# Sliding-window attention followed by an MLP: flat 512-token MLP chunks, paired heads on the two array halves, wide exp and mask, norm ahead of the transpose

## The chip, the core and the metric

The kernel runs on one core of one Trainium2 chip. The metric is the device time of one execution in microseconds (us); less is better. The engines are named as in the profile: PE is TensorE (matmuls and transposes; PEld its weight loads), DVE is VectorE, ACT is ScalarE, POOL is GpSimd and SP is SyncE. [...] POOL and SP also issue the transfers (DMAs), whose packets all run on the same 16 DMA engines.

## The reference

Eight sequences (B = 8) of S = 576 tokens with H = 8 heads of D = 64, so the model width is 512. Attention is causal with a window of 128 and a bias by distance. Its output `x` goes through a layer norm and an MLP of 2048 hidden units, and is added to the result.

```python
scores = scale * np.matmul(q, k.transpose(0, 1, 3, 2))
mask = (rel >= 0) & (rel < window)
scores = np.where(mask, scores + bias[None], -1000000000.0)
...
attn = np.exp(scores)
attn = attn / (np.sum(attn, axis=-1, keepdims=True) + 1e-09)
return np.matmul(attn, v).astype(np.float32)
...
xn = (x - mu) / np.sqrt(var + 1e-06) * g_ln
ch = np.maximum(xn @ w_ch1, 0.0) @ w_ch2
return (x + ch).astype(np.float32)
```

## The kernel before

Tokens lie on the 128 partitions; a sequence of 576 tokens is four blocks of 128 and a tail of 64. The program runs in nine periods: period p does the attention of sequence p (`attn_gen`) and the MLP of sequence p - 1 (`mlp_main`). `drive` interleaves the two generators, and the framework's scheduler then settles each engine's order.

`stage_load` brings q, k and v of a sequence as 15 casting DMAs issued by POOL (fp32 in memory, fp16 on chip), two sequences ahead of need at the start and one ahead later. After the v load, DVE writes the column of ones of the v tile (line 111, `vx`); this write is queued on DVE and cannot run until that tile's transfers have landed.

Attention works on head pairs (`hp`, four a sequence). PE transposes q and k of two heads together (line 136, tile `ptr`), DVE copies them out (line 141, `qt` and `kt`). The scores of one head come from partitions 0 to 63 of these, those of the other from partitions 64 to 127 (line 155, tile `psc`, five matmuls a head, one head after the other). ACT takes the exp of at most 512 columns at a time (lines 163 and 176), DVE multiplies by a banded mask that also holds the bias (lines 169 and 182), and PE forms probabilities times v with a 65th column for the sum (lines 195 and 203, tile `ppv`). DVE normalises (lines 212 to 222) and takes statistics of each head (line 229).

`mlp_pre` combines the statistics on DVE (line 244), subtracts the mean (line 245) and computes the reciprocal root by integer arithmetic and two Newton steps (lines 254 to 285). `mlp_main` transposes (line 297, `pxc`), scales by `g_ln` while copying out on DVE (line 303, `xnt`), multiplies by `w1` for two halves of 288 tokens (line 317, 128 matmuls of 288 columns a sequence), applies relu on ACT or DVE in turn (lines 325 and 329, `ht`), and multiplies by `w2` for five token blocks (line 341, 16 matmuls of 512 columns a block, the last block only 64 tokens wide). DVE scales by the reciprocal root, adds `x` (line 349, `o_tile`), and SP stores.

Of the kernel before, what the change touches and what calls it, by code (L numbers as in the profile page):

```python
# [16 lines left out]
def kernel(  # L17
# [34 lines left out]
    for h in range(H):  # L52
# [21 lines left out]

    x_all = [
        xall_pool.tile([P, NSB, d_model], FP16, tag=f"x{b}", name=f"x_{b}")
        for b in range(B)
    ]

    stage_pool = ctx.enter_context(tc.tile_pool(name="stage", bufs=2))  # L80
    qt_pool = ctx.enter_context(tc.tile_pool(name="qtkt", bufs=2))
    probs_pool = ctx.enter_context(tc.tile_pool(name="probs", bufs=4))
    small_pool = ctx.enter_context(tc.tile_pool(name="small", bufs=4))
    xnt_pool = ctx.enter_context(tc.tile_pool(name="xnt", bufs=2))
    ht_pool = ctx.enter_context(tc.tile_pool(name="ht", bufs=1))
    xc_pool = ctx.enter_context(tc.tile_pool(name="xc", bufs=2))
    out_pool = ctx.enter_context(tc.tile_pool(name="outp", bufs=3))
    sm2_pool = ctx.enter_context(tc.tile_pool(name="sm2", bufs=2))
    att_psum = ctx.enter_context(tc.tile_pool(name="attps", bufs=4, space=bass.MemoryType.PSUM))
    m1_psum = ctx.enter_context(tc.tile_pool(name="m1ps", bufs=2, space=bass.MemoryType.PSUM))  # L90
    m2_psum = ctx.enter_context(tc.tile_pool(name="m2ps", bufs=2, space=bass.MemoryType.PSUM))

    staged = {}
    pre_state = {}

    def stage_load(b):
        qstage = stage_pool.tile([P, NSB, H, D], FP16, tag="qs", name=f"qs{b}")
        kstage = stage_pool.tile([P, NSB, H, D], FP16, tag="ks", name=f"ks{b}")
        vext = stage_pool.tile([P, NSB, H, D + 1], FP16, tag="vx", name=f"vx{b}")
        for src, dst in ((q, qstage), (k, kstage), (v, vext)):  # L100
            for sb in range(NSB):
                pb = pblk(sb)
                nc.gpsimd.dma_start(  # L103
                    out=dst[0:pb, sb, :, 0:D],
                    in_=src[b, :, sb * P : sb * P + pb, :].rearrange(
                        "h p d -> p h d"
                    ),
                )
        nc.vector.memset(qstage[TAIL:P, NSB - 1, :, :], 0.0)
        nc.vector.memset(kstage[TAIL:P, NSB - 1, :, :], 0.0)  # L110
        nc.vector.memset(vext[:, :, :, D : D + 1], 1.0)  # L111
        staged[b] = (qstage, kstage, vext)

    def load_weights():
        w1r = moe_w_ch1.rearrange("(kb p) f -> p kb f", p=P)
        for kb in range(NKB):
            nc.gpsimd.dma_start(out=w1sb[:, kb, :], in_=w1r[:, kb, :])
        w2r = moe_w_ch2.rearrange("(fb p) d -> p fb d", p=P)
        for f0 in range(0, NFB, 4):
            nc.gpsimd.dma_start(out=w2sb[:, f0 : f0 + 4, :], in_=w2r[:, f0 : f0 + 4, :])  # L120

    def attn_gen(b):
        qstage, kstage, vext = staged[b]
        xb = x_all[b]
        stats = sm2_pool.tile(
            [P, NSB, H, nc.vector.BN_STATS_DIM], FP32, tag="stats", name=f"st{b}"
        )
        pre_state[b] = stats
        nc.vector.memset(xb[TAIL:P, NSB - 1, :], 0.0)
        for hp in range(HPAIRS):  # L130
            qt = qt_pool.tile([P, NSB * P], FP16, tag="qt")
            kt = qt_pool.tile([P, NSB * P], FP16, tag="kt")
            for stg, dst in ((qstage, qt), (kstage, kt)):
                ptr = att_psum.tile([P, NSB * P], FP16, tag="att")
                for sb in range(NSB):
                    nc.tensor.transpose(  # L136
                        ptr[:, sb * P : sb * P + P],
                        stg[0:P, sb, 2 * hp : 2 * hp + 2, :],
                        iden[0:P, 0:P],
                    )  # L140
                nc.vector.tensor_copy(out=dst[:, :], in_=ptr[:, :])  # L141
                yield
            probs_2 = []
            for g in range(2):
                h = 2 * hp + g
                r0, r1 = 64 * g, 64 * g + 64
                probs = probs_pool.tile([P, NSB, 2 * P], FP16, tag="probs")
                probs_2.append(probs)
                for jb0 in range(0, NSB, 2):
                    njb = min(2, NSB - jb0)  # L150
                    psc = att_psum.tile([P, 2, 2 * P], FP32, tag="att")
                    for t in range(njb):
                        jbb = jb0 + t
                        nq = 2 * P if jbb < NSB - 1 else P
                        nc.tensor.matmul(  # L155
                            psc[:, t, 0:nq],
                            kt[r0:r1, jbb * P : jbb * P + P],
                            qt[r0:r1, jbb * P : jbb * P + nq],
                            start=True,
                            stop=True,  # L160
                        )
                    if njb == 2:
                        nc.scalar.activation(  # L163
                            out=probs[:, jb0 : jb0 + 2, :],
                            in_=psc[:, :, :],
                            func=AF.Exp,
                            scale=inv_sqrt_d,
                        )
# [191 lines left out]
    def drive(a_gen, b_gen, b_ratio):  # L360
        budget = 0.0
        while a_gen is not None or b_gen is not None:
# [6 lines left out]
            while b_gen is not None and budget >= 1.0:  # L369
                budget -= 1.0  # L370
                try:
                    next(b_gen)
                except StopIteration:
                    b_gen = None

    stage_load(0)
    stage_load(1)
    load_weights()

# [38 lines left out]
```

## Time and profile before

| what | value |
|---|---|
| time, median of 3 runs (lowest, highest) | 465.8 us (465.6, 467.54) |
| span of the profiled execution, first to last instruction | 462.7 us |
| PE busy in the span | 400.8 us (87%) |
| DVE busy | 317.5 us (69%) |
| ACT busy | 129.3 us (28%) |
| POOL busy | 106.4 us (23%) |
| mean granted TensorE clock | 0.954 |

The profiled execution has no time of its own beside its span; the median of the runs lies 3.1 us above that span, which is what lies around the first and the last instruction. Busy PE time is modelled and says little of how close PE is to its best; the starts of successive matmuls say more.

### The profile page before, as it was taken

The page shows a single profiled execution, that of the slowest core. Times are in us where ns is not written, and L with a number is a line of the kernel's source. Part 1 is how long each engine was busy: PE and PEld are TensorE (multiplying, and loading weights), DVE is VectorE, ACT ScalarE, POOL GpSimd, SP SyncE. Part 2 cuts the span into 40 slices and gives each one's busy share as a digit, 9 for nine tenths or more (in the row PEclk, how much of TensorE's full clock was granted, in tenths as well). Part 3 has the DMA queues.
Part 4 walks back from the last instruction along what each step waited for, and adds up shares of the span by engine and source line. Part 5 has one row for each costly group of instructions (what it writes and reads, how often), then busy time and mean ns, then how long its engine had stood idle before and what let it go on. Part 6 is the DMA issues. An engine that isn't in the chain of part 4 may idle for free.

```text
span 462.7 us, 8169 instructions
## 1 busy us (share of the span) xinstructions
PE 400.8 (87%) x3040; PEld 246.4 (53%) x3040; DVE 317.5 (69%) x1362; ACT 129.3 (28%) x321; POOL 106.4 (23%) x132
## 2 busy tenths in 40 slices
PE   1466829996999969997999969997999989998996
PEld 0244516643675447653676447653676456644752
DVE  3469826757787677757778678757878697758331
ACT  1242304500453024420463024420364034500310
POOL 9973510442007300343007300243000000000000
PEclk9999987998899979999799989999799999999999
DMA  9999990599009900299009930299000110011011
GB/s 145 134 161 207 173 54 0 40 135 85 1 1 114 121 24 1 16 134 108 2 1 85 126 47 1 18 133 107 3 1 1 69 36 0 1 70 34 1 45 59
DMA packets 121304, 28.88 MB, mean 62 GB/s; under 512 B 113968, under 2 KB 116016, under 8 KB 121264
## 3 DMA queue, kind: packets, MB, share of 16 engines
q0 software_dynamic: 115200, 18.36, 60.2%
q1 hardware_dynamic: 6064, 10.00, 6.4%
q8 instruction: 24, 0.39, 0.4%
q14 instruction: 16, 0.13, 0.1%
HBM read 37.26 MB, written 9.44 MB: 101 GB/s over the span
## 4 chain that ended last, share of the span: by engine, by line
PE 68%; DMA 11%; POOL 9%; DVE 7%; ACT 2%; issue 2%; POOLq 0%; DVEq 0%
PE psc L155 7%; PE ppv L195 4%; PE ppv L203 3%; DMA ks_544<-in_k_dram 2%; DVE xnt L303 2%; DMA vx_545<-in_v_dram 2%; DMA vx_143<-in_v_dram 2%; DVE o_tile L349 1%; PE pxc L297 1%; ACT ht L325 1%; DMA vx_3477<-in_v_dram 1%; PE ptr L136 1%; DMA vx_1278<-in_v_dram 1%; DMA vx_2011<-in_v_dram 1%; DMA vx_4210<-in_v_dram 1%
## 5 line engine op out<-in xcount | busy, mean ns | idle before, releaser
L317 PEld LDWEIGHTS <-w1sb 128*128 128x128 f16 x1024 | 97.2, 101 | 55.7 <-issue 24.6
L163 ACT ACTIVATE probs<-psc 128x512 f16<-128x512 f32 x128 | 70.5, 603 | 164.4 <-PE psc L155 163.4
L341 PEld LDWEIGHTS <-ht 128*128 128x128 f16 (+1 forms) x640 | 61.7, 100 | 61.3 <-issue 3.4
L169 DVE TENSOR_TENSOR probs<-probs,mband 128x512 f16<-128x512 f16 x128 | 52.1, 419 | 31.9 <-ACT probs L163 26.0
L155 PE MATMUL psc<-qt,kt 64*128 64x256 f16 (+1 forms) x320 | 48.4, 295 | 9.4 <-DVE kt L141 6.8
L155 PEld LDWEIGHTS <-kt 64*128 64x128 f16 x320 | 24.6, 102 | 27.2 <-issue 10.9
L297 PE MATMUL pxc<-iden,xcb 128*128 128x128 f16 (+1 forms) x160 | 16.9, 244 | 23.7 <-DVE xnt L303 21.4
L195 PEld LDWEIGHTS <-probs 128*128 128x128 f16 (+1 forms) x320 | 27.5, 103 | 15.7 <-DVE vx_122 L111 3.2
L303 DVE TENSOR_SCALAR xnt<-pxc,g_sb 128x128 f16<-128x128 f16 (+1 forms) x160 | 32.1, 261 | 0.0
L297 PEld LDWEIGHTS <-xcb 128*128 128x128 f16 (+1 forms) x160 | 11.2, 109 | 31.3 <-issue 27.9
L203 PEld LDWEIGHTS <-probs 128*128 128x128 f16 x256 | 22.8, 105 | 3.0
L141 DVE COPY qt<-ptr 128x640 f16<-128x640 f16 x32 | 15.1, 472 | 7.9 <-PE ptr L136 7.9
L176 ACT ACTIVATE probs<-psc 128x128 f16<-128x128 f32 x64 | 18.8, 294 | 0.0
L141 DVE COPY kt<-ptr 128x640 f16<-128x640 f16 x32 | 15.2, 476 | 3.0 <-PE ptr L136 3.0
L182 DVE TENSOR_TENSOR probs<-probs,mband 128x128 f16<-128x128 f16 x64 | 13.8, 216 | 0.0
L103 POOL DMA_DIRECT2D qs_2742<-in_q_dram x5 | 4.2, 865 | 34.0 <-PE ptr L136 34.0
L212 DVE RECIPROCAL rec<-ppv 128x4 f32<-128x4 f32 x64 | 10.9, 171 | 1.5 <-PE ppv L203 1.4
L103 POOL DMA_DIRECT2D qs_2009<-in_q_dram x5 | 4.2, 856 | 33.1 <-PE ptr L136 33.1
L103 POOL DMA_DIRECT2D qs_4208<-in_q_dram x5 | 4.2, 865 | 32.6 <-PE ptr L136 32.6
L103 POOL DMA_DIRECT2D qs_3475<-in_q_dram x5 | 4.2, 865 | 32.6 <-PE ptr L136 32.6
L136 PE MATMUL ptr<-iden,qs_120 128*128 128x128 f16 x20 | 3.6, 304 | 8.5 <-DMA qs_120<-in_q_dram 8.5
L277 DVE TENSOR_SCALAR hh<-hh 128x5 f32<-128x5 f32 x16 | 3.0, 187 | 11.4 <-DMA vx_1278<-in_v_dram 3.0
(747 smaller groups left out, 835.4 us busy)
## 6 DMA issues: line engine op xcount, KB each, us to landing
out_dram<-o_tile SPq DMA_DIRECT2D x32, 256.0 KB, 2.1
w1sb<-in_moe_w_ch_dram POOLq DMA_DIRECT2D x4, 512.0 KB, 10.8
w2sb<-in_moe_w_ch_dram POOLq DMA_DIRECT2D x4, 512.0 KB, 16.0
out_dram<-o_tile SPq DMA_DIRECT2D x8, 128.0 KB, 2.3
mband<-bandmask SPq DMA_DIRECT2D x1, 512.0 KB, 3.4
qs_120<-in_q_dram POOLq DMA_DIRECT2D x4, 128.0 KB, 4.7
ks_121<-in_k_dram POOLq DMA_DIRECT2D x4, 128.0 KB, 4.9
vx_122<-in_v_dram POOLq DMA_DIRECT2D x4, 128.0 KB, 5.2
```

The costliest lines, as they stand in the source:

```text
L103: nc.gpsimd.dma_start(out=dst[0:pb, sb, :, 0:D], in_=src[b, :, sb * P : sb * P + pb, :].rearrange("h p d -> p h d"),)
L141: nc.vector.tensor_copy(out=dst[:, :], in_=ptr[:, :])
L155: nc.tensor.matmul(psc[:, t, 0:nq], kt[r0:r1, jbb * P : jbb * P + P], qt[r0:r1, jbb * P : jbb * P + nq], start=True, stop=True,)
L163: nc.scalar.activation(out=probs[:, jb0 : jb0 + 2, :], in_=psc[:, :, :], func=AF.Exp, scale=inv_sqrt_d,)
L169: nc.vector.tensor_tensor(out=probs[:, jb0 : jb0 + 2, :], in0=probs[:, jb0 : jb0 + 2, :], in1=mband[:, h, :].unsqueeze(1).broadcast_to([P, ...
L176: nc.scalar.activation(out=probs[:, jb0, 0:P], in_=psc[:, 0, 0:P], func=AF.Exp, scale=inv_sqrt_d,)
L195: nc.tensor.matmul(ppv[:, qb, :], probs[0:kk, qb, 0:P], vext[0:kk, qb, h, :], start=True, stop=(qb == 0),)
L203: nc.tensor.matmul(ppv[:, qb, :], probs[:, qb - 1, P : 2 * P], vext[:, qb - 1, h, :], start=False, stop=True,)
L297: nc.tensor.transpose(pxc[:, kb, 0:pq], xcb[0:pq, tb, kb * P : kb * P + P], iden[0:pq, 0:pq],)
L303: nc.vector.tensor_scalar(out=xnt[:, kb, tb * P : tb * P + pq], in0=pxc[:, kb, 0:pq], scalar1=g_sb[:, kb : kb + 1], scalar2=None, op0=ALU. ...
L317: nc.tensor.matmul(pm1[:, :], w1sb[:, kb, fb * P : fb * P + P], xnt[:, kb, t0 : t0 + HALF], start=(kb == 0), stop=(kb == NKB - 1),)
L341: nc.tensor.matmul(pm2[0:pq, :], ht[:, fb, tb * P : tb * P + pq], w2sb[:, fb, :], start=(fb == 0), stop=(fb == NFB - 1),)
```

## The change

The MLP no longer works by sequence. The tokens of all sequences are one flat row of 4608, cut into nine chunks of 512 (`mlp_gen`): 64 matmuls of 512 columns with `w1`, and four full blocks of 16 matmuls with `w2`. Period c runs the attention of sequence c + 1 and the MLP of chunk c; attention of sequence 0 runs alone ahead of the first, and chunks 7 and 8 run alone at the end.

The two heads' score matmuls are issued in turn, one from partitions 0 to 63 and one from 64 to 127. The 1024 columns of a head pair that belong together go through one exp and one mask multiply, with a single score tile (`sc`, one buffer of two banks). q and k arrive as fp32 through SP's queue, six DMAs a head pair into four rotating buffers, and DVE casts them (line 190). v still comes through POOL's casting DMAs, into two lasting tiles whose ones and zeros are written once. The statistics are taken over all 512 columns, ACT computes the reciprocal root by ln and exp, the norm is applied before the transpose (line 303), and ACT copies the transposed blocks out (line 321, `xt`). `g_ln` is multiplied into `w1` once by DVE (`scale_w1`). For odd sequences two DMAs shift `x` to the flat layout.

```diff
-        for src, dst in ((q, qstage), (k, kstage), (v, vext)):
-            for sb in range(NSB):
-                nc.gpsimd.dma_start(
...
-        nc.vector.memset(vext[:, :, :, D : D + 1], 1.0)
...
+    GRP = [0, 0, 1, 1, 1]
+    OFF = [0, 256, 256, 0, 192]
+    NQ = [256, 256, 256, 192, 64]
+    ORDER = [[0, 1], [3, 4, 2]]
...
+    def load_qk(b, hp):
+        i = (b * HPAIRS + hp) % NSTG
+        for src, dst in ((q, q32[i]), (k, k32[i])):
+            s = src[b, 2 * hp : 2 * hp + 2, :, :]
+            for g in range(2):
+                nc.sync.dma_start(
+                    out=dst[:, 0:NFULL, g, :],
+                    in_=s[g, 0 : NFULL * P, :].rearrange("(sb p) d -> p sb d", p=P),
+                )
...
+    nc.gpsimd.tensor_copy(m2g[:, :, 0:192], mband[:, :, 0:192])
+    nc.gpsimd.tensor_copy(m2g[:, :, 192:256], mband[:, :, 0:64])
+    nc.gpsimd.tensor_copy(m2g[:, :, 256:512], mband[:, :, :])
...
+    def scale_w1():
+        for f0 in range(0, ffn, 512):
+            for kb in range(NKB):
+                nc.vector.tensor_scalar(
+                    out=w1sb[:, kb, f0 : f0 + 512],
...
+                s16 = st16_pool.tile([P, NSB, P], FP16, tag=f"{nm}16")
+                nc.vector.tensor_copy(
+                    out=s16[:, :, :], in_=stg[:, :, :, :].rearrange("p s h d -> p s (h d)")
+                )
...
+            for grp in range(2):
+                sc = sc_psum.tile([P, 2, 512], FP32, tag="sc")
+                for j in ORDER[grp]:
+                    for g in range(2):
+                        r0 = D * g
                         nc.tensor.matmul(
...
+                nc.scalar.activation(
+                    out=probs[:, :, :], in_=sc[:, :, :], func=AF.Exp, scale=inv_sqrt_d
+                )
...
-                for tb in range(NSB):
-                    nc.vector.bn_stats(
-                        out=stats[:, tb, h, :], in_=xb[:, tb, D * h : D * h + D]
-                    )
...
+            nc.vector.bn_stats(out=st[0:pq, :], in_=xb[0:pq, tb, :])
+            nc.vector.bn_aggr(out=mv[0:pq, tb, :], in_=st[0:pq, :])
...
+            pxt = att_psum.tile([P, NKB, P], FP16, tag="att")
...
+                nc.scalar.activation(
+                    out=xt_of(c)[:, :, col : col + n],
...
+            for kb in range(NKB):
+                nc.tensor.matmul(
+                    pm[:, :],
+                    w1sb[:, kb, fb * P : fb * P + P],
+                    xt[:, kb, :],
...
+    load_weights()
+    load_v_all(1)
+    scale_w1()
+    drive(attn_gen(0), None, 0.0)
+    for c in range(NCHUNK):
+        drive(attn_gen(c + 1) if c + 1 < B else None, mlp_gen(c), 1.0)
```

The scheduler's order at three places follows. The first is DVE's queue during the first head pair of sequence 0. Before the change it held masks (lines 169 and 182), the ones of `vx_122` and the normalising steps:

```order
L169 TENSOR_TENSOR probs<-probs,mband 128x512 x2
L182 TENSOR_TENSOR probs<-probs,mband 128x128
L111 MEMSET vx_122 128x40
L169 TENSOR_TENSOR probs<-probs,mband 128x512
L212 RECIPROCAL rec<-ppv 128x4
L169 TENSOR_TENSOR probs<-probs,mband 128x512
L182 TENSOR_TENSOR probs<-probs,mband 128x128
```

With the change, the same stretch of DVE's queue reads as follows (`s_200` and the like are the fp16 casts, `dst` the copied transposes, `m2g` the rearranged mask):

```order
L190 CAST s_200<-q_0_100 128x640
L190 CAST s_210<-k_0_104 128x640
L199 COPY dst<-ptr 128x640 x2
L190 CAST s_270<-q_1_101 128x640
L225 TENSOR_TENSOR probs<-probs,mband 128x1024
L190 CAST s_280<-k_1_105 128x640
L234 TENSOR_TENSOR probs<-probs,m2g 128x1024
L160 TENSOR_SCALAR w1sb<-w1sb,g_sb 128x512 x16
L263 RECIPROCAL rec<-ppv 128x5 x2
L264 TENSOR_TENSOR xp_199<-ppv,rec 128x5x64 x2
L190 CAST s_340<-q_2_102 128x640
```

All 16 scalings of `w1` now stand between the second mask and the first normalisation of sequence 0.

The second is POOL's queue at the start. Before, the weights stood behind 30 loads of q, k and v (two rows for each tile, of which the last tile's are shown):

```order
L103 DMA vx_143<-in_v_dram 128x8x64 x4
L103 DMA vx_143<-in_v_dram 64x8x64
L117 DMA w1sb<-in_moe_w_ch_dram 128x2048 x4
L120 DMA w2sb<-in_moe_w_ch_dram 128x4x512 x4
L103 DMA qs_543<-in_q_dram 128x8x64 x4
```

With the change they stand behind the five loads of v of sequence 0, and the last quarter of `w1` also behind the three mask copies:

```order
L118 DMA vx_116<-in_v_dram 128x8x64 x4
L118 DMA vx_116<-in_v_dram 64x8x64
L153 DMA w1sb<-in_moe_w_ch_dram 128x4x512 x3
L139 COPY m2g<-mband 128x8x192
L140 COPY m2g<-mband 128x8x64
L141 COPY m2g<-mband 128x8x256
L153 DMA w1sb<-in_moe_w_ch_dram 128x4x512
L155 DMA w2sb<-in_moe_w_ch_dram 128x4x512 x4
L118 DMA vx_117<-in_v_dram 128x8x64 x4
```

The weights moved ahead of all loads but one tile's.

The third is DVE's queue in a period. Before, in the first shared period, the ones of `vx_545` stood ahead of the normalisation of sequence 1 (`x_77`):

```order
L212 RECIPROCAL rec<-ppv 128x4
L213 RECIPROCAL rec<-ppv 64x1
L329 TENSOR_SCALAR ht<-pm_717 128x288
L111 MEMSET vx_545 128x40
L216 TENSOR_TENSOR x_77<-ppv,rec 128x4x64
L222 TENSOR_TENSOR x_77<-ppv,rec 64x64
```

With the change no such write is left, and the end of a period reads as follows on DVE (`xo_548` is `x` of sequence 1):

```order
L264 TENSOR_TENSOR xo_548<-ppv,rec 128x5x64 x2
L363 TENSOR_TENSOR o_tile<-pm,xp_199 128x512
L287 BN_STATS st<-xo_548 128x6 x2
L288 BN_AGGR mv<-st 128x2
L287 BN_STATS st<-xo_548 128x6
L288 BN_AGGR mv<-st 128x2
L287 BN_STATS st<-xo_548 128x6
L288 BN_AGGR mv<-st 128x2
L287 BN_STATS st<-xo_548 64x6
L288 BN_AGGR mv<-st 128x2
L363 TENSOR_TENSOR o_tile<-pm,xp_199 128x512
L288 BN_AGGR mv<-st 64x2
```

Statistics and norm of a whole sequence now follow its last head in one piece.

## Rows read from the trace of the kernel before

**Rows 1.** Page, busy time, share and instructions of PE.

```profile
PE 400.8 (87%) x3040; PEld 246.4 (53%) x3040; DVE 317.5 (69%) x1362; ACT 129.3 (28%) x321; POOL 106.4 (23%) x132
```

**Rows 2.** Stretches: busy time of each engine, granted clock, DMA engines busy, GB/s.

```profile
0.00:68.60 68.60, 33.76 (x256) 20.92 (x257) 38.82 (x195) 14.95 (x35) 43.23 (x57) 0.97 2.06 147
...
164.00:217.00 53.00, 49.46 (x380) 30.55 (x380) 39.19 (x170) 15.96 (x40) 12.66 (x15) 0.94 0.59 57
372.00:421.00 49.00, 47.18 (x382) 29.29 (x382) 38.40 (x167) 15.85 (x40) 0.00 (x0) 1.00 0.07 25
421.00:462.70 41.70, 35.13 (x229) 21.53 (x228) 15.42 (x42) 6.56 (x16) 0.00 (x0) 0.98 0.10 32
```

**Rows 3.** Waits of the whole span: total us, times, longest.

```profile
PE pxc L297 <- DVE xnt L303: 21.4, 10, 3.9
...
DVE x_77 L216 <- DMA vx_545<-in_v_dram: 9.6, 1, 9.6
```

**Rows 4.** The chain that ended last: start, us, what.

```profile
451.42 3.45 PE pm_5952 L341 x16
...
458.48 0.74 DVE o_tile L349
```

**Rows 5.** Timeline of PE inside a period: start, us, instruction, count.

```profile
226.93 0.44 PE L136 MATMUL ptr<-iden,qs_2009 128*128 128x128 f16 x5
227.21 0.33 PE L136 MATMUL ptr<-iden,ks_2010 128*128 128x128 f16 x3
...
230.73 0.66 PE L155 MATMUL psc<-qt,kt 64*128 64x256 f16 x5
231.33 0.66 PE L317 MATMUL pm_2983<-xnt,w1sb 128*128 128x288 f16 x4
...
233.51 0.22 PE L195 MATMUL ppv<-vx_2011,probs 128*128 128x65 f16 x2
...
233.81 0.20 PE L195 MATMUL ppv<-vx_2011,probs 64*128 64x65 f16 x1
...
233.99 0.66 PE L317 MATMUL pm_3036<-xnt,w1sb 128*128 128x288 f16 x4
234.48 0.65 PE L317 MATMUL pm_3042<-xnt,w1sb 128*128 128x288 f16 x4
```

**Rows 6.** Timeline of PE, sequence 0 alone and a period's first matmuls.

```profile
24.25 1.14 PE L155 MATMUL psc<-qt,kt 64*128 64x256 f16 x7 [2.11 <-DVE kt L141]
...
31.12 1.14 PE L155 MATMUL psc<-qt,kt 64*128 64x256 f16 x7 [2.00 <-DVE kt L141]
...
222.81 1.15 PE L317 MATMUL pm_2858<-xnt,w1sb 128*128 128x288 f16 x4
223.75 1.17 PE L317 MATMUL pm_2864<-xnt,w1sb 128*128 128x288 f16 x4
```

**Rows 7.** Groups of ACT by form: busy us, mean ns of one, idle before.

```profile
L163 ACT ACTIVATE probs<-psc 128x512 f16<-128x512 f32 x128 | 70.5, 603 | 164.4 <-PE psc L155 163.4 <-PE pxc L297 0.9
L176 ACT ACTIVATE probs<-psc 128x128 f16<-128x128 f32 x64 | 18.8, 294 | 0.0
```

**Rows 8.** Groups of DVE by form in 217 to 270 us.

```profile
L169 DVE TENSOR_TENSOR probs<-probs,mband 128x512 f16<-128x512 f16 x16 | 6.6, 420 | 3.3 <-ACT probs L163 3.0
L229 DVE BATCH_NORM_STATS2 st_2763<-x_80 128x6 f32<-128x64 f16 x40 | 5.7, 206 | 0.0
L216 DVE TENSOR_TENSOR x_80<-ppv,rec 128x256 f16<-128x256 f32 x8 | 3.3, 418 | 0.0
L141 DVE COPY kt<-ptr 128x640 f16<-128x640 f16 x4 | 1.9, 474 | 0.0
...
L182 DVE TENSOR_TENSOR probs<-probs,mband 128x128 f16<-128x128 f16 x8 | 1.7, 218 | 0.0
...
L244 DVE BATCH_NORM_AGGREGATE mv<-st_2763 128x2 f32<-128x48 f32 x5 | 1.5, 336 | 0.0
L212 DVE RECIPROCAL rec<-ppv 128x4 f32<-128x4 f32 x8 | 1.4, 172 | 0.0
```

More of the change, by code (lines that the diff above doesn't have):

```diff
@@ L80 @@
[L80 to L87, printed above, removed]
@@ L114, in load_weights @@
+    w1r = moe_w_ch1.rearrange("(kb p) f -> p kb f", p=P)
+    w2r = moe_w_ch2.rearrange("(fb p) d -> p fb d", p=P)
     def load_weights():
[L115 to L118, printed above, removed]
+        for f0 in range(0, ffn, 512):
+            nc.gpsimd.dma_start(out=w1sb[:, :, f0 : f0 + 512], in_=w1r[:, :, f0 : f0 + 512])
@@ L245, in mlp_pre @@
+        yield
+        for tb in range(NSB):
+            pq = P if tb < NFULL else TAIL
+            if tb < NFULL:
+                xs = xs_pool.tile([P, d_model], FP16, tag="xs")
+            else:
+                xs = xs_tail[b % 2]
             nc.vector.tensor_scalar(
-                out=xcb[0:pq, tb, :],
+                out=xs[0:pq, :],
                 in0=xb[0:pq, tb, :],
                 scalar1=mv[0:pq, tb, 0:1],
-                scalar2=None,
+                scalar2=rstd[0:pq, tb : tb + 1],
@@ L250, in mlp_pre @@
                 op0=ALU.subtract,
+                op1=ALU.mult,
             )
[L252 to L263 removed]
@@ new lines, in attn_gen, with mlp_gen @@
+            t0 = b * S + tb * P
+            done = 0
+            while done < pq:
+                c, col = divmod(t0 + done, CH)
+                n = min(pq - done, CH - col)
+                nc.scalar.activation(
+                    out=xt_of(c)[:, :, col : col + n],
+                    in_=pxt[:, :, done : done + n],
+                    func=AF.Copy,
+                )
+                done += n
+            yield
+    def mlp_gen(c):
+        xt = xts[c]
+        ht = ht_pool.tile([P, NFB, CH], FP16, tag="ht")
+        for fb in range(NFB):
+            pm = mm_psum.tile([P, CH], FP32, tag="mm")
+            for kb in range(NKB):
+                nc.tensor.matmul(
+                    pm[:, :],
+                    w1sb[:, kb, fb * P : fb * P + P],
+                    xt[:, kb, :],
+                    start=(kb == 0),
+                    stop=(kb == NKB - 1),
+                )
+            if fb % 4 != 3:
+                nc.scalar.activation(out=ht[:, fb, :], in_=pm[:, :], func=AF.Relu)
+            else:
+                nc.vector.tensor_scalar(
+                    out=ht[:, fb, :], in0=pm[:, :], scalar1=0.0, scalar2=None, op0=ALU.max
@@ L376 @@
-    stage_load(0)
-    stage_load(1)
-    load_weights()
-    for period in range(B + 1):
-        a_gen = attn_gen(period) if period < B else None
-        m_gen = mlp_main(period - 1) if period >= 1 else None
-        if 1 <= period and period + 1 < B:
-            stage_load(period + 1)
-        drive(a_gen, m_gen, 42.0 / 24.0)
-        if period < B:
-            mlp_pre(period)
+        while a_gen is not None or m_gen is not None:
+            if a_gen is not None and next(a_gen, StopIteration) is StopIteration:
+                a_gen = None
+            budget += ratio if a_gen is not None else 1e9
+            while m_gen is not None and budget >= 1.0:
+                budget -= 1.0
+                if next(m_gen, StopIteration) is StopIteration:
+                    m_gen = None
```

386 lines of the change are left out of this document (164 added, 222 removed).

## The prediction

> **What bounds the kernel now.** I read the page first: PE is busy 87% of the span [rows 1], so I looked for the stages in which it is not, and then for the starts of its matmuls. The table by stretches shows three parts [rows 2]. Up to 68.6 us loads rule: 147 GB/s, and PE busy only half the time. The seven shared periods follow, of which 53.0 us is a typical one and 49.0 us the last, with no loads under it. The MLP of the last sequence alone takes 41.7 us to the end.
>
> Inside a period PE streams: four matmuls of 288 columns start 0.49 us before the next four, five transposes 0.28, five score matmuls 0.60, and nine value matmuls 0.48 (233.51 to 233.99), of which the last two, with the 64-token tail, take 0.18 [rows 5]. Sixteen matmuls of 512 columns take 3.45 us [rows 4]. So a sequence costs PE 128/4 x 0.49 = 15.7 for `w1`, 5 x 3.45 = 17.3 for `w2`, 8 x 0.28 = 2.2, 8 x 0.60 = 4.8, 8 x 0.48 = 3.8 and some 1.2 for transposing `x`: 45 us. The 49 to 53 measured hold 4 to 8 us of waits. Two are plain in the list of waits [rows 3]: PE's `x` transposes wait for DVE's copies (21.4 us), and DVE once stood 9.6 us on the load of v, since its write of ones is queued ahead of the normalisation. [...]
>
> **The change, PE's part.** `w1` now takes 64 matmuls of 512 columns a chunk and `w2` 64, all at 3.45/16 = 0.216 us: 27.6 us a period. That is less than 15.7 + 17.3 partly because a period has 512 tokens, not 576; what is truly saved is the half-empty fifth `w2` block of each sequence (576 instead of 640 such matmuls, 13.8 us in all). In `w1`, 288 columns already run at 0.49/4/288 = 0.43 ns a column, as 512 do, so the wider form gains nothing.
>
> [...]
>
> Scores: with both heads in turn, do the two halves of the array run side by side? [...] A head pair then costs 1024 columns at 0.43 = 0.44 us. Entering or leaving the 64-row form costs 0.60 - 1152 x 0.43 = 0.11 us, four times a pair: 0.88 in all, 3.5 us a period. If they did not overlap it would be 5.3.
>
> Value matmuls: the tail is padded to 128 rows, so nine run at the pace of the first seven (0.30/7 = 0.043): 0.39 a head, 3.1 a period. Transposes stay: 2.2 and 20 x 0.056 = 1.1. PE's sum for a period is 27.6 + 3.5 + 3.1 + 2.2 + 1.1 = 37.5 us.
>
> **Waits inside a period.** I follow one head pair along the new order, with four or so MLP matmuls (0.86 us) between its steps. The exp of 1024 columns costs, by the slope of its two forms, 603 + 512 x (603 - 294)/384 = 1015 ns [rows 7]. With one score buffer the second score group waits for the first exp. Behind the scores' end lie about 0.2 us of hand-over and, in the first half of a period, up to 0.3 of a relu already in ACT's queue; covered are five matmuls, 1.08. So 0.3 us is lost in the `w1` half and 0.1 in the other. The second mask costs 420 + 512 x (420 - 218)/384 = 690 ns by the same slope [rows 8]; from the second scores to the value matmuls that need it go 0.2 + 1.02 + 0.69 + 0.1 = 2.0 us, and cover is seven or nine matmuls (1.5 or 1.9) and six value matmuls: 0.2 lost. For the next pair, `kt` comes out behind a copy (0.474), a cast and sometimes a relu. The cast of 640 fp32 columns has no row: between 0.4 (a 16-bit operation of 512 columns takes 0.420) and 0.8 (one column a ns, as the 256 columns of line 216); I take 0.5, as fixed cost makes up much of each row. The loss is 0.2 on average, nothing to 0.5. Together 0.55 a pair, 2.2 a period.
>
> At a period's end the statistics come in one piece. From the last value matmul: two reciprocals and two multiplies (2 x 0.17 + 2 x 0.52, the latter 0.418 for 256 columns, scaled to 320), an output sum (0.75), five statistics at 0.206 + 448 x 0.98 ns = 0.64 (0.98 being line 216's slope over line 212), four combinations of at most 0.336, say 0.2, then ln and exp of at most 0.294 each with hand-overs, and the norm, at most 0.42: about 7.3 us. PE has 28 matmuls to do meanwhile, 6.0. So 1.3 us is lost, and another 1.0 as five transposed blocks leave through ACT at 0.6 each with two buffers. Period: 37.5 + 2.2 + 2.3 = 42.0 us.
>
> What hides the rest: ACT has eight exps, twelve relus and five copies, 8.1 + 7.2 + 3.3 = 19 us of 42; DVE has some 31 us by the rows above, so it too has slack, though not much. Loads: fp32 q and k of a sequence are 2.4 MB, v 0.6 and stores 1.0; in 42 us that is 95 GB/s against the 147 sustained at the start [rows 2], and four q/k buffers keep a whole sequence of lead. Without that cover, each microsecond of a late load would stop the cast and all that is queued behind it on DVE.
>
> **The start.** DVE cannot normalise head pair 0 until all of `w1` has landed and been scaled, for the 16 scalings stand ahead of it in its queue. Until then must land v (0.6 MB as written), `w1` (2.1), q and k of sequence 0 (2.4) and the mask (0.5): 5.6 MB, at 147 GB/s 38 us, less if SP's transfers are cheaper. I take 37, with 25 (POOL's share alone, 2.7 MB, from 1.2 us on, at somewhat less than that pace) and 47 (a quarter more) as bounds; POOL's three mask copies delay only the last quarter of `w1` and lie inside these. Then come four scalings (at most 1.7) and, at the low clock level, the chain of each pair: normalise 1.4, cast and copies 1.5, scores 0.63, exp 1.02, scores 0.63, exp 1.02, mask 0.74, values 0.86: 7.8 us. Before, pairs of sequence 0 followed each other in 6.87 us [rows 6]; the single score buffer explains the longer one. Pairs 1 to 3 end at 38.7 + 1.4 + 3 x 7.8 = 63.5; five statistics and combinations (4.2), ln and exp (0.8), norm (0.4), four transposes and hand-over (0.6) and four copies at 0.6 add 8.4. The MLP starts at about 72.0, against 68.6 now.
>
> **The sum.** 72.0 + 3.2 (clock still low at first) + 7 x 42.0 + two chunks alone 2 x 27.6 + the last sum and store 4.2 (458.48 to the span's end, [rows 4]) = 428.6 us of span. Against the old span of 462.7: start +3.4, periods 294 + 3.2 against 352.4, end 59.4 against 41.7. The median of the runs is 3.1 us above the profiled span, so 432 us.
>
> **Rivals.** (a) Everything hides: waits of 1 us a period and `w1` at 25 us give 432 - 7 x 3.5 - 12 = 395, either alone 407 or 420. For it: loads through SP may be lighter. Against: the one-piece statistics. (b) The chain of a head pair binds: a cast and mask at one column a ns (0.8 and 1.2) make DVE late four times a period, 4.5 us more: 463. Against it: lines 169 and 182 show half a ns a column for 16-bit masks. [...]
>
> [...]
>
> **How the numbers follow.** Forecast 0.56 (417 to 447, with `w1` late or the scores in file), (a) 0.14, (b) 0.12, (c) 0.12, (d) 0.06. The range 402 to 460 leaves out the best of (a), most of (b) and (d). A change of 0.5%, about what a measurement of this kernel can tell, is 463.5 to 468.1. Faster are the forecast, (a), (c) and half of (b), 0.89; the same 0.05, slower 0.06.
>
> **What would show it.** The 512-column matmuls at 0.216; score pairs of 0.44 us side by side; DVE idle until `w1` lands near 37 us; first MLP matmul near 72; periods of 42 us with PE's waits at the second scores, the late value matmuls and the first `pxt`. Wrong would be periods above 47 us, a granted clock under 0.9 in them, or a start past 85.

## The result, and the profile after

The changed kernel takes 402.94 us (median of 4 runs, 402.39 to 404.31) against 465.7: a ratio of 0.866, with a 95% interval of 0.863 to 0.870. That is 62.8 us less, and 29 less than the 432 forecast: just inside the range of 402 to 460, but outside the 417 to 447 of the forecast proper. The profiled span is 400.6 us. The page gives PE's busy time, share and instructions, to set beside [rows 1]:

```profile
PE 337.4 (84%) x2528; PEld 167.5 (42%) x2528; DVE 227.2 (57%) x543; ACT 154.7 (39%) x249; POOL 43.7 (11%) x55
```

The stretches, with the columns of [rows 2]: start, a typical period, and the two last chunks alone.

```profile
0.00:75.80 75.80, 18.39 (x178) 13.07 (x179) 32.08 (x92) 12.74 (x18) 22.70 (x30) 1.00 1.21 172
190.10:228.10 38.00, 37.72 (x305) 18.55 (x302) 26.58 (x64) 18.21 (x29) 4.20 (x5) 1.00 0.64 114
341.40:400.60 59.20, 55.41 (x257) 24.95 (x255) 11.76 (x17) 14.33 (x24) 0.00 (x0) 1.00 0.11 41
```

A period has PE busy for 37.72 of 38.00 us, at a granted clock of 1.00, where a typical period of before had 0.94 [rows 2]. In the start the 1.00 is not the pace of PE, as its first `w1` matmuls show:

```profile
75.76 1.62 PE L335 MATMUL pm<-xt_514,w1sb 128*128 128x512 f16 x4
77.22 0.44 PE L195 MATMUL ptr<-iden,s_566 128*128 128x128 f16 x5
```

These four take 1.46 us, 1.7 times the 0.86 of later ones. The first `w1` matmuls of the nine chunks start at 75.76, 114.32, 152.28, 190.10, 228.07, 265.84, 303.81, 341.39 and 369.02. So the forecast's sum can be checked term by term:

| term | forecast | measured |
|---|---|---|
| start, to the first MLP matmul | 72.0 | 75.76 |
| low clock after it | 3.2 | 0.7 (first period 38.56 against 37.8; 0.6 of it at these four) |
| seven periods | 294 | 264.9 (37.6 to 38.0 each) |
| two chunks alone, last sum and store | 59.4 | 59.2 |
| outside the span | 3.1 | 2.3 |

The error is the period. Where it went is read from PE's timeline (start, us, instruction, count), to set beside [rows 5]:

```profile
192.53 1.25 PE L335 MATMUL pm<-xt_1572,w1sb 128*128 128x512 f16 x5
193.87 0.40 PE L212 MATMUL sc<-dst 64*128 64x192 f16 x6
...
199.60 0.39 PE L212 MATMUL sc<-dst 64*128 64x256 f16 x4
199.92 1.25 PE L335 MATMUL pm<-xt_1572,w1sb 128*128 128x512 f16 x5
201.11 0.40 PE L212 MATMUL sc<-dst 64*128 64x192 f16 x6
201.43 0.82 PE L335 MATMUL pm<-xt_1572,w1sb 128*128 128x512 f16 x3
...
203.11 0.19 PE L255 MATMUL ppv<-vx_116,probs 128*128 128x65 f16 x1
203.35 0.20 PE L246 MATMUL ppv<-vx_116,probs 128*128 128x65 f16 x1
203.39 0.20 PE L255 MATMUL ppv<-vx_116,probs 128*128 128x65 f16 x1
...
218.48 6.20 PE L353 MATMUL pm<-w2sb,ht 128*128 128x512 f16 x28
224.55 0.66 PE L313 MATMUL pxt<-iden,xs 128*128 128x128 f16 x7
```

Five matmuls of 512 columns at 0.216 are 1.08 us; from 199.92 to 201.11 they took 1.19, of which 0.1 is the entry into the 64-row form (a step into it takes 0.12 in the run with the unpadded tail, below): these second scores waited for almost nothing. Those at 193.87 came 1.34 us behind the same five matmuls, so they waited 0.16. The late value matmuls waited 0.2 (203.11 to 203.35), and then follow each other at 0.03. At the period's end PE streams 28 matmuls in 6.07 us and goes straight on to the first transposes of `xs`. DVE's timeline there:

```profile
218.50 0.38 DVE L263 RECIPROCAL rec<-ppv 128x5 f32<-128x5 f32 x2 [0.45 <-PE ppv L255]
218.79 0.85 DVE L264 TENSOR_TENSOR xp_2129<-ppv,rec 128x320 f16<-128x320 f32 x2
219.55 0.68 DVE L363 TENSOR_TENSOR o_tile<-pm,xp_1076 128x512 f32<-128x512 f32 x1
220.15 1.28 DVE L287 BATCH_NORM_STATS2 st<-xp_2129 128x6 f32<-128x512 f16 x2
...
223.40 0.65 DVE L363 TENSOR_TENSOR o_tile<-pm,xp_1076 128x512 f32<-128x512 f32 x1
...
224.08 1.38 DVE L303 TENSOR_SCALAR xs<-xp_2129,mv,rstd 128x512 f16<-128x512 f16 x4
```

From the reciprocals to the first norm's end DVE takes 6.0 us, as long as the 28 matmuls.

For the records of PE in one period, the time from each start to the next, summed by line, gives what each kind of work costs. A wait, or an entry into the 64-row form, counts with the instruction ahead of it, which is mostly an MLP matmul:

| us a period | before (222.81 to 275.06) | after (190.10 to 228.07) |
|---|---|---|
| `w1` matmuls | 17.50 | 14.83 |
| `w2` matmuls | 17.84 | 14.41 |
| scores | 5.20 | 2.61 |
| values | 4.12 | 2.65 |
| transposes of q and k | 2.68 | 2.23 |
| transposes of `x` | 4.93 | 1.22 |

The forms with no row before came out as follows (groups of the page: busy us, mean ns, idle before), beside [rows 7, 8]:

```profile
L220 ACT ACTIVATE probs<-sc 128x1024 f16<-128x1024 f32 x64 | 65.4, 1022 | 97.4 <-PE sc L212 97.4
L225 DVE TENSOR_TENSOR probs<-probs,mband 128x1024 f16<-128x1024 f16 x32 | 22.1, 692 | 33.7 <-ACT probs L220 33.7
L199 DVE COPY dst<-ptr 128x640 f16<-128x640 f16 x64 | 31.1, 488 | 8.6 <-PE ptr L195 8.5
```

The forecast had 1015 for the exp and 690 for the mask.

At the start the order is another than forecast. DVE's timeline:

```profile
17.98 0.58 DVE L190 CAST s_270<-q_1_101 128x640 f16<-128x640 f32 x1 [5.71 <-DMA q_1_101<-in_q_dram]
...
25.67 0.49 DVE L190 CAST s_280<-k_1_105 128x640 f16<-128x640 f32 x1 [6.51 <-DMA k_1_105<-in_k_dram]
...
28.20 4.39 DVE L160 TENSOR_SCALAR w1sb<-w1sb,g_sb 128x512 f16<-128x512 f16 x16 [1.44 <-DMA g_sb<-in_moe_g_ln_dram]
...
32.73 0.89 DVE L264 TENSOR_TENSOR xp_199<-ppv,rec 128x320 f16<-128x320 f32 x2
...
40.87 0.50 DVE L190 CAST s_350<-k_2_106 128x640 f16<-128x640 f32 x1 [4.52 <-DMA k_2_106<-in_k_dram]
...
51.60 0.85 DVE L264 TENSOR_TENSOR xp_199<-ppv,rec 128x320 f16<-128x320 f32 x2
...
59.11 0.85 DVE L264 TENSOR_TENSOR xp_199<-ppv,rec 128x320 f16<-128x320 f32 x2
...
66.89 0.85 DVE L264 TENSOR_TENSOR xp_199<-ppv,rec 128x320 f16<-128x320 f32 x2
```

Pair 0 was held first by the loads of pair 1: its two masks stand behind casts of pair 1's q and k, at which DVE stood 5.71 and 6.51 us. The 16 scalings ran at 28.20 to 32.6, so `w1` was there ahead of 37, and what they waited for, 1.44 us, was the load of `g_sb`. Pair 1 was then normalised 18.9 us after pair 0 (51.60 and 32.73), since casts for pairs 2 and 3 stand ahead of its copies and masks and wait for their loads. Pairs 2 and 3 follow at 7.5 and 7.8, the rhythm forecast.

### The profile page after: what moved, and what is told of

Read it like the earlier page. It is cut to its first block, busy times and chain, and to the rows that moved or that the text cites. A ratio compares the mean times of both kernels' runs of the same rounds, so it can differ in the third digit from the quotient of the medians.

```text
span 400.6 us, 6433 instructions
## 1 busy us (share of the span) xinstructions
PE 337.4 (84%) x2528; PEld 167.5 (42%) x2528; DVE 227.2 (57%) x543; ACT 154.7 (39%) x249; POOL 43.7 (11%) x55
## 4 chain that ended last, share of the span: by engine, by line
PE 68%; ACT 12%; SPq 8%; DMA 5%; DVE 5%; issue 1%; DVEq 0%
PE pm L353 29%; PE pm L335 24%; ACT probs L220 9%; PE ptr L195 4%; SPq L93 4%; PE sc L212 4%; SPq L97 3%; PE pxt L313 3%; DMA k_2_106<-in_k_dram 3%; ACT ht L343 3%; PE ppv L246 3%; DVE probs L234 3%; PE ppv L255 2%; DMA q_0_100<-in_q_dram 2%; DVE st L287 1%
## 5 line engine op out<-in xcount | busy, mean ns | idle before, releaser
L353 PE MATMUL pm<-w2sb,ht 128*128 128x512 f16 x576 | 138.6, 379 | 0.0
L220 ACT ACTIVATE probs<-sc 128x1024 f16<-128x1024 f32 x64 | 65.4, 1022 | 97.4 <-PE sc L212 97.4
L343 ACT ACTIVATE ht<-pm 128x512 f16<-128x512 f32 x108 | 64.6, 598 | 75.8 <-PE pm L335 75.8
L353 PEld LDWEIGHTS <-ht 128*128 128x128 f16 x576 | 51.5, 98 | 50.3 <-issue 1.5
L335 PEld LDWEIGHTS <-w1sb 128*128 128x128 f16 x576 | 48.9, 98 | 47.5 <-issue 5.0
L246 PEld LDWEIGHTS <-probs 128*128 128x128 f16 x320 | 25.5, 101 | 43.0 <-DVE probs L234 19.7
L345 DVE TENSOR_SCALAR ht<-pm 128x512 f16<-128x512 f32 x36 | 24.8, 688 | 29.7 <-PE pm L335 29.7
L212 PE MATMUL sc<-dst 64*128 64x256 f16 (+2 forms) x320 | 26.9, 264 | 15.4 <-DVE dst L199 9.7
L199 DVE COPY dst<-ptr 128x640 f16<-128x640 f16 x64 | 31.1, 488 | 8.6 <-PE ptr L195 8.5
L212 PEld LDWEIGHTS <-dst 64*128 64x128 f16 x320 | 12.2, 97 | 41.3 <-DVE dst L199 22.6
L118 POOL DMA_DIRECT2D vx_117<-in_v_dram x20 | 16.9, 866 | 108.2 <-PE ppv L255 102.0
L118 POOL DMA_DIRECT2D vx_116<-in_v_dram x20 | 16.9, 865 | 104.0 <-PE ppv L255 103.2
L335 PE MATMUL pm<-xt_514,w1sb 128*128 128x512 f16 x64 | 17.0, 390 | 0.0
L335 PE MATMUL pm<-xt_546,w1sb 128*128 128x512 f16 x64 | 16.4, 380 | 0.0
```

The source lines that it names most:

```text
L118: nc.gpsimd.dma_start(out=dst[0:pb, sb, :, 0:D], in_=v[b, :, sb * P : sb * P + pb, :].rearrange("h p d -> p h d"),)
L212: nc.tensor.matmul(sc[:, g, OFF[j] : OFF[j] + NQ[j]], kt[r0 : r0 + D, j * P : j * P + P], qt[r0 : r0 + D, j * P : j * P + NQ[j]], start=Tr ...
L220: nc.scalar.activation(out=probs[:, :, :], in_=sc[:, :, :], func=AF.Exp, scale=inv_sqrt_d)
L246: nc.tensor.matmul(ppv[:, qb, :], pr[GRP[qb]][:, g, OFF[qb] : OFF[qb] + P], vx[:, qb, h, 0 : D + 1], start=True, stop=(qb == 0),)
L335: nc.tensor.matmul(pm[:, :], w1sb[:, kb, fb * P : fb * P + P], xt[:, kb, :], start=(kb == 0), stop=(kb == NKB - 1),)
L343: nc.scalar.activation(out=ht[:, fb, :], in_=pm[:, :], func=AF.Relu)
```

## The experiments

All are compared with the kernel before; the changed kernel's 402.94 is the mark for those made from it. The kernel before had medians of 463.9 to 466.2 us beside them, so a difference of some 2 us from 402.94 says little by itself.

**Order of the two heads' scores.**

```diff
-                for j in ORDER[grp]:
-                    for g in range(2):
+                for g in range(2):
+                    for j in ORDER[grp]:
```

> The changed kernel with the two heads' score matmuls one after the other instead of in turn. Theory A (the turn-taking is what lets the halves of the array work together): a pair costs 2048 columns at 0.43 ns instead of 1024, 0.44 us more, so the score stretches go from 0.32 to about 0.55 us and the time from 402.9 to about 415 us (28 pairs under the MLP at 0.44, four at the low clock level at 0.85). Theory B (PE takes matmuls of the other half out of a run in file too, as the seven neighbours of the kernel before hinted): a difference under 3 us.

403.44 us (ratio 0.863 to 0.868), no change, as theory B has it: four score matmuls take 0.33 us in this order too. The alternation in the code is not what makes them overlap.

**The two heads' work apart.** Each head with its own score tile (two buffers of 512 columns), exp and mask of 512 columns, and MLP matmuls between the heads (`drive` is set to hand out MLP matmuls at 32/38 of its rate, as a pair has more steps):

```diff
-                sc = sc_psum.tile([P, 2, 512], FP32, tag="sc")
...
+                for g in range(2):
+                    r0 = D * g
+                    sc = sc_psum.tile([P, 512], FP32, tag="sc")
+                    for j in ORDER[grp]:
...
+                    yield
...
-        drive(attn_gen(c + 1) if c + 1 < B else None, mlp_gen(c), 1.0)
+        drive(attn_gen(c + 1) if c + 1 < B else None, mlp_gen(c), 32.0 / 38.0)
```

> The changed kernel with the two heads' work taken apart again: each head has its own score tile of one bank (two buffers), its own exp and mask of 512 columns, and its turn for MLP matmuls before the next head's scores. Theory E (the pairing matters because neighbours run side by side on PE, and each group pays its own entry and exit): of the 0.65 us a pair, 1024 columns at 0.42 ns become 2048, 0.44 us more, and two further entries and exits of 0.11 us each time, 0.44 us: 28 pairs in the periods at 0.9 us are 25 us, 425 to 432. Rival F (the wait for the exp that the single wide buffer causes, 0.25 us a pair, goes away, and neighbouring groups still overlap now and then): 0.5 us a pair, 412 to 420. Rival G (the pairing is hidden behind waits anyway): 400 to 406, periods of 38 us.

418.5 us (418.31 to 419.44), 15.6 more: rival F's band. A typical period is 40.59; scores take 4.53 of it instead of 2.61, 0.5 a pair as F has it, and transposes of `x` 2.01 instead of 1.22; its second score buffer brings the first MLP matmul forward to 73.20. PE's timeline of this run:

```profile
198.16 0.39 PE L213 MATMUL sc<-dst 64*128 64x256 f16 x2
198.48 0.39 PE L332 MATMUL pm<-xt,w1sb 128*128 128x512 f16 x1
198.80 0.39 PE L213 MATMUL sc<-dst 64*128 64x256 f16 x2
199.12 1.04 PE L332 MATMUL pm<-xt,w1sb 128*128 128x512 f16 x4
```

One head's two matmuls hold PE for 0.32 us, as long as both heads' four at 199.60 of the changed kernel. So neighbours on the two halves do run side by side, and it is being neighbours that counts. The run changes more than that, so not all of the 15.6 us is the pairing: of the 0.8 more at the transposes, 0.4 is a wait for ACT, where no MLP matmuls are left to stand between them:

```profile
234.44 0.72 PE L310 MATMUL pxt<-iden,xs 128*128 128x128 f16 x8
235.52 0.87 PE L310 MATMUL pxt<-iden,xs 128*128 128x128 f16 x8 [0.36 <-ACT xt L318]
```

**The 64-token tail of the values unpadded.**

```diff
+                    kk = P if qb < NFULL else TAIL
...
-                        pr[GRP[qb]][:, g, OFF[qb] : OFF[qb] + P],
-                        vx[:, qb, h, 0 : D + 1],
+                        pr[GRP[qb]][0:kk, g, OFF[qb] : OFF[qb] + P],
+                        vx[0:kk, qb, h, 0 : D + 1],
```

> The changed kernel with the value matmul of the tail block over 64 rows of probabilities and v, as before, instead of 128 padded rows. Theory A (each change between 64 and 128 rows drains PE): two changes a head, 0.09 to 0.18 us a head more, 56 heads under the MLP and 8 alone, so 407 to 414 us. Theory B (the switch hides behind the waits for the mask): 403.

415.86 us (414.79 to 416.34), 12.9 more: theory A, a little above its band. A period is 39.64, and values take 4.32 of it instead of 2.65. PE's timeline:

```profile
203.29 0.19 PE L256 MATMUL ppv<-vx,probs 128*128 128x65 f16 x1
203.41 0.20 PE L247 MATMUL ppv<-vx,probs 64*128 64x65 f16 x1
203.54 0.20 PE L256 MATMUL ppv<-vx,probs 128*128 128x65 f16 x1
203.58 0.20 PE L247 MATMUL ppv<-vx,probs 128*128 128x65 f16 x1
```

The step into the 64-row matmul and the step out cost 0.12 and 0.13 us, where neighbours in one form stand 0.03 apart: 0.2 us a head, 12.8 for 64 heads. What PE does in these steps is not shown.

**Matmuls of 256 columns for `w1`.**

```diff
+            for c0 in range(0, CH, 256):
...
-                    xt[:, kb, :],
+                        xt[:, kb, c0 : c0 + 256],
```

> The changed kernel with each w1 matmul of 512 columns cut into two of 256 (twice the matmuls and weight loads, the same columns and the same relus). The prediction's claim (256 columns already stream at full pace, so the wide form by itself gains nothing): 403 to 406 us, about 0.002 us for each of the 576 added matmuls. Rival (a weight load for every 256 columns is no longer hidden, since a load takes 0.098 us and the columns 0.109): over 410 us.

404.33 us (403.81 to 405.25), ratio 0.866 to 0.871, in the band of the claim. The median hides part of the cost: the first MLP matmul starts at 73.73, 2.0 us earlier than in the changed kernel, for a reason that stays open. Periods grow by 0.3 and a chunk alone from 27.63 to 27.79; from the first MLP matmul to the end this run takes 328.5 us instead of 324.8. So the width alone gives little, some 3.6 us or 0.9%, but 0.006 us for each added matmul instead of the 0.002 expected.

**Two score buffers**, and two instead of four for the MLP's results:

```diff
-    sc_psum = ctx.enter_context(tc.tile_pool(name="scps", bufs=1, space=bass.MemoryType.PSUM))
+    sc_psum = ctx.enter_context(tc.tile_pool(name="scps", bufs=2, space=bass.MemoryType.PSUM))
...
-    mm_psum = ctx.enter_context(tc.tile_pool(name="mmps", bufs=4, space=bass.MemoryType.PSUM))
+    mm_psum = ctx.enter_context(tc.tile_pool(name="mmps", bufs=2, space=bass.MemoryType.PSUM))
```

> The changed kernel with two score tiles (four banks) and two MLP accumulators instead of one and four. Theory A (the single score buffer costs 0.15 us a pair as PE waits for the first exp): about 5 us less, 398. Theory B (the wait only moves, to the value matmuls that need the second mask): 402 to 404. Rival C (with two accumulators PE waits for relus and output sums): slower, above 406.

399.54 us (399.03 to 400.21), between theories A and B. Most of the gain is at the start: the first MLP matmul runs at 73.41, 2.4 us earlier. Periods are 37.66, 0.3 less, half of what theory A has for them; a chunk alone takes 0.3 more.

**The kernel before with the ones of v written once**, into two lasting tiles:

```diff
-        vext = stage_pool.tile([P, NSB, H, D + 1], FP16, tag="vx", name=f"vx{b}")
+        vext = vext_2[b % 2]
...
-        nc.vector.memset(vext[:, :, :, D : D + 1], 1.0)
```

> The kernel before with two lasting v tiles whose column of ones is written once, so that DVE's queue no longer holds a write that waits for the load of v. Theory A (the start-of-period stalls and the low clock after them come from that queued write): the five periods with loads shrink from 52 or 53 to about 49.5 us and the first loses part of its 9.6 us stall, so 465.7 goes to 440 to 450 us. Theory B (the loads of q, k and v are late anyway, and the value matmuls wait for v as long): within 5 us of 465.7.

439.73 us (438.19 to 440.19), ratio 0.947: 25 us less than the 464.56 of the kernel before beside it, from one edit, at the best end of theory A. Its granted clock averages 0.983 against 0.954, its first shared period takes 50.8 us instead of 64.8, the later ones mostly 49 to 51 instead of 51 to 53.

**The start, five ways.** First, `w2`'s loads wait on POOL until pair 0 is normalised:

```diff
+        nc.gpsimd.tensor_copy(w2sb[:, 0:NFB:4, 0:2], gate)
```

> The changed kernel with the four loads of w2 held back until head pair 0 of sequence 0 is normalised (a small copy on POOL ahead of them waits for it); the v of sequence 1 moves ahead of them. Theory A (the start is bound by the 16 DMA engines: q and k of pairs 2 and 3 share them with the weights): 2.1 MB as written leave the first 31 us, at about 170 GB/s some 10 us earlier for the k of pair 2, so the MLP starts near 65 instead of 75.8 us and the time is near 393 us. Theory B (SP's own issuing of six loads a pair is the limit): k of pair 2 still lands at 40 us, and the time stays within 2 us of 403. Theory C (the scaling of w1 holds DVE): no change either.

401.02 us (400.88 to 402.13), first MLP matmul at 73.93. The time is what theory B has, but not for its reason. DVE's timeline:

```profile
32.74 0.49 DVE L193 CAST s<-k 128x640 f16<-128x640 f32 x1 [0.72 <-DMA k<-in_k_dram]
...
47.10 0.49 DVE L193 CAST s<-q 128x640 f16<-128x640 f32 x1 [7.20 <-DMA q<-in_q_dram]
```

The k of pair 2 is cast at 32.74 instead of 40.87, so without `w2` the loads come sooner, as theory A has it. But `w2`, now issued from 31.78 us on, holds up a load of sequence 1, whose cast stands ahead of pair 1's second mask. Second, the scalings behind sequence 0's attention in the code:

```diff
-    scale_w1()
     drive(attn_gen(0), None, 0.0)
+    scale_w1()
```

> The changed kernel with the 16 scalings of w1 written after the attention of sequence 0, so that the scheduler spreads them over its idle time instead of putting all ahead of the first normalisation. Theory C of the prediction (DVE cannot go on until w1 is scaled): the MLP starts 5 to 8 us earlier, 395 to 398 us. Theory A (DVE then waits for the q and k of pair 2, landing at 40.9 us, whether or not it has scaled w1): 402 to 404 us.

398.81 us (398.49 to 399.31), first MLP matmul at 71.16: 4.1 us less, nearer to theory C than to A. Third, identity and mask through ACT's queue, all weights gated, the scalings on POOL:

```diff
-    nc.sync.dma_start(out=mband, in_=m_dram.ap())
+    nc.scalar.dma_start(out=mband, in_=m_dram.ap())
...
+        nc.gpsimd.tensor_copy(w1sb[:, 0, 0:ffn:512], gate)
...
-                nc.vector.tensor_scalar(
+                nc.gpsimd.tensor_scalar(
```

> The start of the changed kernel reordered: the identity and the mask are issued from ACT's queue, the loads of w1 and w2 wait for a POOL copy that reads x of head pair 0 of sequence 0, and POOL instead of DVE multiplies g_ln into w1. Theory C (the 75.8 us before the first MLP matmul are lost to the order of loads: 4.2 MB of weights share the DMA engines with q, k and v of sequence 0, and casts of later pairs hold DVE's queue): pairs of sequence 0 can begin some 10 us sooner and follow each other in 7.8 us, the first MLP matmul starts at 55 to 62 us, and the time falls by as much, to 383 to 391. Rival D (the weights merely arrive later, and POOL's 16 scalings, which have no row, take about 1 us or more each): the first MLP matmul stays at 71 to 78 us and the time at 398 to 406. The periods stay at 37.9 us under both.

397.34 us (397.08 to 397.92), first MLP matmul at 70.22: far from theory C and just under rival D's band. Pair 0 was normalised at 18.87 us instead of 32.73, but then the weights, issued from 19.9 us on, slowed SP's queue, and pair 1 followed only at 33.66. Two of SP's issues in this run's timeline, 2 and 6 us after the first weights were issued:

```profile
21.93 0.71 SPq L97 DMA_DIRECT2D k<-in_k_dram  x1
...
26.07 3.21 SPq L97 DMA_DIRECT2D q<-in_q_dram  x1
```

DVE's timeline shows where that arrives, at casts of later loads (the first of them stands ahead of pair 1's normalisation):

```profile
33.03 0.49 DVE L192 CAST s<-k 128x640 f16<-128x640 f32 x1 [7.01 <-DMA k<-in_k_dram]
...
40.63 0.52 DVE L192 CAST s<-q 128x640 f16<-128x640 f32 x1 [5.18 <-DMA q<-in_q_dram]
...
49.19 0.53 DVE L192 CAST s<-k 128x640 f16<-128x640 f32 x1 [7.64 <-DMA k<-in_k_dram]
```

Fourth, the same with two score buffers and two accumulators.

> The same reordered start, and two score buffers of two banks each instead of one, with two buffers instead of four for the MLP's results. If the two gains are independent (two score buffers alone gave 399.5, that is 3.4 us), the time is that of the run with the reordered start less 3 to 4 us: 380 to 388 under theory C, 395 to 403 under rival D. If the score wait at the start and the late loads cover each other, less than 1.5 us is gained over the reordered start alone.

392.13 us (391.33 to 393.46): 5.2 less than without, so the two gains add up, with some more at the start (first MLP matmul at 66.86). Fifth, `w1` gated on pair 1 and `w2` on pair 2, the scalings on DVE between the masks:

```diff
-    for _ in range(6):
+    for _ in range(12):
...
+    load_w2(xbatch[0][:, 0, 4 * D : 4 * D + 4])
+    scale_w1([0])
...
+    scale_w1(range(512, ffn, 512))
```

> The reordered start with two score buffers, but w1 is loaded only once x of head pair 1 of sequence 0 is written (about 27 us), w2 only once that of pair 2 is, and DVE does the scaling again, in pieces between the masks of pairs 2 and 3. In the run before it, weights that began at 19.9 us made each of SP's issues take 3.2 us instead of 1.1, and DVE stood 7.0, 5.2 and 7.6 us at casts of pair 3 and of sequence 1. Theory C in its narrower form (the weights' transfers slow the q and k loads that are under way, and casts that stand two pairs ahead in DVE's queue pass that on): pairs 0 to 2 keep a rhythm of 7.5 to 7.8 us, the first MLP matmul starts at 55 to 61 us instead of 66.9, and the time is 381 to 386. Rival (the 8 MB that must land by then rule, whatever their order: at 176 GB/s 45 us, and scalings that wait for w1 now hold DVE instead): 65 us or later, 390 to 396.

385.43 us (384.89 to 386.5), ratio 0.829 (0.826 to 0.833), the fastest here. (The waits of 7.0, 5.2 and 7.6 us named above are those of the third way; the fourth had 4.9, 6.6 and 5.5.) The first MLP matmul starts at 58.18 instead of 66.86, and time and start lie in the band of the narrower theory. Its rhythm does not: pairs are normalised at 19.84, 27.50, 39.23 and 48.88, since now scalings that wait for `w1`, 7.0 us in all, hold DVE, which the rival had foreseen. One of them:

```profile
34.93 0.61 DVE L164 TENSOR_SCALAR w1sb<-w1sb,g_sb 128x512 f16<-128x512 f16 x2 [2.69 <-DMA w1sb<-in_moe_w_ch_dram]
```

The first period then takes 41.5 us, since casts of sequence 1 still wait for loads issued while `w2` was under way, 3.2 us at the longest:

```profile
59.07 0.49 DVE L194 CAST s<-k 128x640 f16<-128x640 f32 x1 [3.19 <-DMA k<-in_k_dram]
```

## Why the prediction was right, and what was off

**PE's work was right but for the values.** The sum was 37.5 us a period. A chunk alone takes 27.63 (27.6 forecast); scores 2.61 and eight entries of 0.10, 3.4 (3.5), since the two heads' matmuls overlap, on which the 0.44 us a pair rests (four take 0.33 us, one head's two 0.32); transposes 2.2 and 1.2 (2.2 and 1.1). Values were mis-sized: the forecast took 0.30/7 = 0.043 for each matmul of the padded form. They follow each other at 0.03, 2.2 a period instead of 3.1. The 0.30 held the step into the 64-row form (0.12), and the unpadded run shows that the two steps around the 64-row form hold the rest.

**The step that failed is "Waits inside a period": 2.2 in the pairs and 2.3 at the end, 4.5 us.** Measured on the starts in the period at 190.10, what PE loses beyond its own pace is 0.3 at the second scores (twice 0.16; the other six enter at once), 0.56 at late value matmuls and 0.29 between the transposes of `xs`: some 1.2, so 3.3 less than forecast. With the values' 0.9 that makes the 4.1 us by which the period was forecast too long, 29 us over seven. With two score buffers all eight score groups enter at once; the period there is 0.3 shorter, which fits, though late values (0.47) and the output sums moved a little too. Three mistakes stand behind it. At the end of a period I added up the durations on DVE, 7.3, but starts lie closer than durations say: the two multiplies took 0.76 (218.79 to 219.55) and not 1.04, the output sum 0.60 and not 0.75, five statistics with their combinations 3.25 (220.15 to 223.40) and not 4.0; and ln and exp ran beside the output sum at 223.40. Of the 1.0 us for five blocks through ACT with two buffers only 0.29 was lost, because `w2` matmuls stand between those transposes; with the heads apart, where none were left, the transposes took 0.8 more. And the 0.55 a pair took all hand-overs at their longest in every pair: 0.22 was measured.

**The clock and the rivals.** The granted clock was 1.00 in the stretches shown, at a period's end and within it, so the two rivals on the clock, (c) and (d), did not come about. No run shows the 3.2 us that the sum adds for a clock still low at first, nor the low clock level that it takes for a head pair at the start: the first period took 38.56 us against 37.8, 0.7 more, in the start the granted clock read 1.00 while four matmuls took 1.46 us instead of 0.86, and pairs 2 and 3 followed at 7.5 and 7.8 us. Rival (b) fell on its own terms: the cast takes 0.49 and the mask 0.69, not 0.8 and 1.2. Rival (a), waits of 1 us a period, was the nearest to the truth: its 407 without the early `w1` is 4 us above the result, for the reason that it named. So the forecast's mechanism is right in PE's work and wrong in the waits, and that 402.94 still lies within the range, by 0.9 us, is luck.

**The start was right in size (72.0 against 75.76) and half wrong in mechanism.** The scalings do block DVE, but only from 28.2 to 32.6, and not because `w1` was late; moving them gave 4.1 us of time. The rest is loads of q and k. While weights and v are loading, at 187 to 199 GB/s between 10 and 40 us, SP's issues grow from 0.6 us to 3 and at most 6.0, and the casts that the scheduler set one or two pairs ahead on DVE hold up the pair in hand: 12.2 us before pair 0 was masked, 10.2 us more before pair 1 was. Where the weights were held back the slow issues moved with them (one took 3.21 us at 26.07 in the third way, with the weights issued from 19.9 us on, and one 3.21 at 36.47 in the fifth, where `w1` waited for pair 1, normalised at 27.50); why an issue then takes so long is not shown. Moving the weights behind pair 1, with the other edits of the start and two score buffers, brought the first MLP matmul 17.6 us forward.

**Where the 62.8 us come from.** The prediction put the MLP's start in the kernel before at 68.6. That is a misreading: it is the end of PE's wait behind the late `v`, and the MLP had begun before it. PE's timeline of before:

```profile
52.67 1.12 PE L317 MATMUL pm_659<-xnt,w1sb 128*128 128x288 f16 x4
...
68.66 1.12 PE L317 MATMUL pm_763<-xnt,w1sb 128*128 128x288 f16 x4 [8.76 <-DVE ht L329]
...
424.95 0.65 PE L317 MATMUL pm_5700<-xnt,w1sb 128*128 128x288 f16 x4 [0.49 <-DVE xnt L303]
```

Measured alike, from the first MLP matmul on, the spans differ by +23.1 us at the start (52.67 to 75.76), -106.7 in the seven shared periods (372.3 to 265.6, the first of them 64.8 to 38.56) and +21.5 at the end (37.8 to 59.2, where two chunks now stand alone): 62.1 in all. So the change lost at the start what the runs above partly win back.

A typical period shrank by 14.3 us (52.25 to 37.97). By the table of starts the MLP's share is 6.1, of which 5.4 was forecast (33.0 to 27.6) and comes with 512 tokens instead of 576 and no half-empty block; scores 2.6, values 1.5, transposes of `x` 3.7, of q and k 0.5. Most of the 5.4 is moved, not saved: nine chunks of 27.6 are 249 us, eight sequences of 33.0 were 264. Single edits bear out three of the parts: taking the heads apart costs 15.6 us in all, the unpadded tail 12.9, and the ones of v alone give the kernel before 25. The MLP's own share, the norm ahead of the transpose and ACT's copies were not tried by a run of their own, and how far the single edits overlap stays open.

## What to carry to other kernels

Sum a stage from the starts of instructions, not from their durations, on every engine in a chain, and ask of each wait what the scheduler can put into it. Where two heads share the array's halves, keep their matmuls neighbours (here four took 0.33 us, two alone 0.32) and pad odd tails to the form around them: the steps into the 64-row form and out of it cost 0.12 and 0.13 us. A cast, scale or memset on a shared engine is a wait on its data's load, up to 7.6 us on DVE here; put it behind the work in hand, and hold bulk loads back until the small ones on the critical chain are through.

## What the runs showed of the hardware beyond that

PE ran the two heads' matmuls side by side although one head's stood wholly behind the other's in its queue (0.33 us for four in either order; one head's two take 0.32, so in strict order four would need about 0.43, an estimate by half the 0.216 of 512 columns). By that estimate PE did not take these strictly in the order of its queue. The pace of 512-column matmuls stayed at 13.81/64 = 0.216 us with nothing else on PE. On POOL, 16 scalings of 128x512 took 25.5 us, 1.6 each, against 4.4 us for all on DVE.
